# Query and key rows of the dilated heads: eight neighbouring positions to a partition, one load for a head and tensor, and copies that write every second column

## The chip, the cores and the metric

The kernel runs on one core of one Trainium2 chip. The metric is the time of the device in microseconds (us). Five engines take part: TensorE (PE, with its weight loads as PEld), VectorE (DVE), ScalarE (ACT), GpSimd (POOL) and SyncE (SP), whose queue here does nothing but issue loads and stores.

## The reference

Three layers follow each other. Attention over 4 batches, 8 heads, 576 positions and 64 columns a head: the first four heads of a batch look back over 32 neighbouring positions, the last four, the dilated heads, over 32 positions at distance 4. Then a layer of 2048 hidden units with a rational function, then eight experts, each with 1024 hidden units, mixed by a gate that is normalised in turns.

```
rel = pos[:, None] - pos[None, :]
mask_plain = (rel >= 0) & (rel < window)
mask_dil = (rel >= 0) & (rel < window * dilation) & (rel % dilation == 0)
masks = np.stack([mask_plain if h < H // 2 else mask_dil for h in range(H)], axis=0)
scores = np.where(masks[None, :, :, :], scores, -1000000000.0)
...
h = x @ w_in
...
return (g @ w_out).astype(np.float32)
...
out += P[:, e:e + 1] * ye
```

## The kernel before

Attention works on pairs of heads: pair 0 and 1 of a batch are plain, pair 2 and 3 are dilated. For one pair the columns of both heads fill the 128 partitions of `qT` and `kT`, and the 576 positions lie along the free axis. In the dilated pairs the positions are ordered by their remainder by 4, the 144 positions of one remainder behind each other, so that the 32 positions which a query looks at are neighbours. With that order the same code computes plain and dilated pairs.

The way there, for a pair: `att_load` (L266 to L290) loads q and k with positions on the partitions. `att_prep` (L338 to L366) turns them: four steps a pair, x = 0 and 1 for the two halves of q, x = 2 and 3 for those of k; a step is three or four transposes on TensorE into a bank `qkps` (L356) and one copy by ScalarE into `qT` or `kT` (L364), which for a dilated pair also puts the positions in order. `att_qk` adds mask (L372) and products (L379) in a bank `scps`; VectorE takes the maximum (L397), ScalarE three exponentials (L399), VectorE and GpSimd the division (L403 to L405). `att_tr` transposes the result (L414, copy L419), `att_av` multiplies with v (L438), and ScalarE and VectorE split the output into two f16 parts (L229, L232).

For a dilated pair a load of before takes 72 partitions of four neighbouring positions each, that is half of the 576 positions of one head: four loads for q (two heads, two halves) and four for k (L286). In a half the remainder of a position is its place within the partition, and the copy writes runs of 72 neighbouring columns.

Batch 0 is computed first, as a list of pieces (`run_piece`), with other work hung in between (`extra`): the loads and the conversion of the first two column blocks of `w_in` (`wi_load`, L166; `wi_conv`, where ScalarE's L501 is the first to read a loaded piece, then VectorE's L505 to L507 and ScalarE's L536), the scan of v for its maximum (L493), and `wg_prep` (L595), which reads the small load `wgr` (L1324). The second layer begins with the first matmuls L640 to L642. Batches 1 to 3 are worked in pieces between the steps of the second layer.

What sets the order: each engine works through its own queue in order and waits at the first instruction whose inputs are missing. The order itself is made when the program is built, by a list scheduler that works with priorities and with its own estimates of when an input arrives; so a change of a load can move instructions on every engine. SP issues one load after another. Loads carry one of eight counters in turn, and a load waits until the load eight places earlier, with the same counter, has landed.

Of the kernel before, what the change touches and what calls it, by code (L numbers as in the profile page):

```python
# [10 lines left out]
F32 = mybir.dt.float32  # L11
# [17 lines left out]
def kernel(  # L29
# [14 lines left out]
    nc = tc.nc  # L44
    B, H, S, D = q.shape
# [12 lines left out]
    QB = 96  # L58
    KW = 96
    GQ = 192  # L60
    HS = S // 2
    CL = S // 4
    HSTR = S * D
# [47 lines left out]
    def room(tag, shape, dt):  # L111
        where, era, a, size = HOME[tag]
        n = math.prod(shape[1:]) * (2 if dt == F16 else 4)
        assert n <= size, (tag, shape)
        old = rooms.get(where)
        if old is None or old[0] < era:
            old = rooms[where] = era, sb.tile([P, ROOMS[where] // 4], F32R if era == 1 else F32, tag=where, name=f"room{where}")
        assert old[0] == era, (tag, old[0])
        t = old[1][0:shape[0], a // 4:(a + n) // 4]
        if dt != (F32R if era == 1 else F32):  # L120
            t = t.bitcast(dt)
        d = "abcd"[:len(shape) - 1]
        if len(d) > 1:
            t = t.rearrange(f"p ({' '.join(d)}) -> p {' '.join(d)}", **dict(zip(d[1:], shape[2:])))
        return t
# [5 lines left out]
    def bank(name, long=False):  # L131
        bank_n[0] += 1
        if spare_banks[0] and bank_n[0] % 2:
            long = True
        return psum.tile([P, 512], F32, tag="long" if long else "bank", bufs=4, name=name)
# [104 lines left out]
    ident = cpool.tile([P, P], F32, name="ident")  # L240
# [11 lines left out]
    for i, x in enumerate(SEAMS):  # L252
        if x is None:
            continue
        m = masks[:, i, 0:32 + x]
# [11 lines left out]
    def att_load(b, pr, stage=None):  # L267
        off = (b * H + 2 * pr) * HSTR
        st = att.setdefault((b, pr), {})
        if stage:  # L270
            both = room(stage, [P, 2, 1024], F32)
        for i, (src, tag) in enumerate(((q, "aq"), (k, "ak"))):
            if stage:
                w, n = (QB, 6) if pr < 2 else (72, 8)
                t = both[:w, i, 0:n * 2 * D].rearrange("p (c h d) -> p c h d", c=n, h=2)
            elif pr < 2:
                t = room(tag, [QB, 6, 2, D], F32)
            else:
                t = room(tag, [72, 8, 2, D], F32)
            if pr < 2:  # L280
                for h in range(2):
                    nc.sync.dma_start(out=t[:, :, h, :], in_=bass.AP(src.tensor, off + h * HSTR, [[D, QB], [QB * D, 6], [1, D]]))
            else:
                for h in range(2):
                    for y in range(2):
                        nc.sync.dma_start(  # L286
                            out=t[:, 4 * y:4 * y + 4, h, :],
                            in_=bass.AP(src.tensor, off + h * HSTR + y * HS * D, [[4 * D, 72], [D, 4], [1, D]]),
                        )
            st[tag] = t  # L290

    NG = H // 2 * 3

# [36 lines left out]
    def att_qk_tiles(alt):  # L330
        if alt:
            t = room("W3", [P, 2 * S + 32], F32)
            qT, kT = t[:, 0:S], t[:, S:]
        else:
            qT = room("aqT", [P, S], F32)
            kT = room("akT", [P, S + 32], F32)
        nc.vector.memset(kT[:, 0:32], 0.0)
        return qT, kT  # L338

    def att_prep(b, pr, x):  # L340
        st = att[b, pr]
        which, y = divmod(x, 2)
        key = "ak" if which else "aq"
        src = st[key]
        alt = b < 2 and pr % 2
        if x == 0:
            if ("qkT", alt) not in att:
                att["qkT", alt] = att_qk_tiles(alt)
            st["qT"], st["kT"] = att["qkT", alt]
        d = st["kT"][:, 32:] if which else st["qT"]  # L350
        if y == 1:
            st.pop(key)
        w, n = (QB, 3) if pr < 2 else (72, 4)
        bt = bank("qkps")
        for c in range(n):
            nc.tensor.transpose(bt[:, c * w:(c + 1) * w], src[:, n * y + c, :, :].rearrange("p h d -> p (h d)"), ident[:w, :w])  # L356

        def after():
            if pr < 2:
                dv, ps = d[:, y * HS:(y + 1) * HS], bt[:, 0:HS]  # L360
            else:
                dv = d.rearrange("m (c w) -> m c w", c=4)[:, :, y * 72:(y + 1) * 72]
                ps = bt[:, 0:HS].rearrange("m (c p) -> m c p", c=4)
            nc.scalar.activation(dv, ps, AF.Copy, scale=1.0 if which else QSCALE)  # L364

        return after  # L366
# [804 lines left out]
    def run_piece(pc):  # L1171
        kind, b, pr, x = pc
        flush()
        if kind == "prep":
            after.append(att_prep(b, pr, x))
            if x == 3:
                for a in LOADS.get((b, pr), ()):
                    att_load(*a)
        elif kind == "qk":
            after.append(att_qk(b, pr, x))  # L1180
        elif kind == "tr":
            after.append(att_tr(b, pr, x))
        else:
            after.append(att_av(b, pr, x))
            g = b * NG + 3 * pr + x
            if g < 4 or g >= 8:
                att_load_v(g + 8 if g < 4 else g + 4)
# [15 lines left out]
    for b, s0, s1 in ATT:  # L1203
        pcs = att_pieces(b)
        n = 4 * (s1 - s0 + 1) - 4
# [103 lines left out]


    att_load(0, 0)
    for i in range(2):
        att_load_v(i)
    att_load(0, 1, "R1")
    nc.sync.dma_start(out=abt[:, 0:4], in_=ra.partition_broadcast(P))
    nc.sync.dma_start(out=abt[:, 4:6], in_=rb.partition_broadcast(P))
# [16 lines left out]
    n = len(pcs)  # L1333
# [96 lines left out]
```

## Time and profile before

| what | value |
|---|---|
| three runs | 1989.99, 1990.22, 1991.6 us; median 1990.22 us |
| the profiled execution, its own time | 1990.97 us |
| its span in the trace | 1989.0 us |
| TensorE busy | 1892.8 us (95%) |
| VectorE busy | 1574.9 us (79%) |
| ScalarE busy | 1217.4 us (61%) |
| GpSimd busy | 494.5 us (25%) |

The profiled execution lies 0.75 us above the median, and 1.97 us of it lie outside the span. TensorE's busy share is 95% over the whole, but in the page's row of forty slices (49.7 us each) it reads 6 and 6 tenths in the first two, 8 in the third and fourth and 9 from the fifth on, apart from three 8s. The time that TensorE does not work lies mostly at the beginning.

### The profile page before, as it was taken

To read this page: it belongs to the slowest core of one execution; us is meant where nothing else is said; L and a number is where in the kernel's file an instruction comes from. 1 tells how busy PE (TensorE), PEld (TensorE's weight loads), DVE (VectorE), ACT (ScalarE), POOL (GpSimd) and SP (SyncE) were. 2 spreads that over 40 slices of the span, in tenths; PEclk is the share of its full clock that TensorE was granted. 3 is DMA by queue.
4 is the path that set the end of the run, shared out by engine and by line. 5 is a ranking of instruction groups with operands and counts; after the bars stand their busy time and mean duration, and the time that the engine had idled before them with its cause. 6 is when DMAs were issued, how large, how long until landed. Compare 5 with 4: busy or idle time off the path is not lost. (4 is left out here: it accounts for less than half of the span.)

```text
span 1989.0 us, 36639 instructions
## 1 busy us (share of the span) xinstructions
PE 1892.8 (95%) x14202; PEld 1420.9 (71%) x14202; DVE 1574.9 (79%) x2564; ACT 1217.4 (61%) x2182; POOL 494.5 (25%) x489
## 2 busy tenths in 40 slices
PE   6688999999989999999999999999999999999998
PEld 5466676776767677777777777777777777777777
DVE  4696899789997999788778877868877787787764
ACT  4776777776675645656655655555565565565552
POOL 1132234232232104013311411411321141142111
PEclk6689999999999999999999999999999999999999
DMA  6643221124310352465356256335434734543323
GB/s 170 166 139 92 50 71 34 32 63 148 99 43 22 122 172 75 131 176 169 76 119 180 64 118 161 78 82 138 130 60 119 184 65 109 158 93 75 85 59 54
DMA packets 213518, 207.93 MB, mean 105 GB/s; under 512 B 78816, under 2 KB 161248, under 8 KB 213344
## 3 DMA queue, kind: packets, MB, share of 16 engines
q1 hardware_dynamic: 196480, 173.09, 29.2%
q0 software_dynamic: 16864, 32.51, 10.9%
q8 instruction: 111, 1.82, 0.4%
q14 instruction: 63, 0.52, 0.1%
HBM read 155.86 MB, written 49.68 MB: 103 GB/s over the span
## 5 line engine op out<-in xcount | busy, mean ns | idle before, releaser
L930 PEld LDWEIGHTS <-roomA 128*128 128x128 f16 x3276 | 319.6, 98 | 177.1 <-issue 10.1
L930 PE MATMUL l1a<-roomA 128*128 128x384 f16 x1872 | 356.6, 326 | 1.2 <-ACT roomV L979 0.9
L930 PE MATMUL l1b<-roomA 128*128 128x384 f16 x1404 | 273.6, 326 | 3.4 <-DVE roomA L981 1.8
L686 POOL TENSOR_TENSOR roomIG<-roomA,roomIG 128x384 fp32r<-128x384 f32 x96 | 116.4, 1224 | 238.8 <-ACT roomIG L685 217.5
L1030 PE MATMUL yps<-roomA 128*128 128x256 f16 x630 | 169.9, 273 | 2.2 <-DVE roomV L1056 1.5
L1030 PE MATMUL yps<-roomA,roomV 128*128 128x256 f16 x630 | 168.7, 273 | 2.5 <-DVE roomA L1053 1.1
L1031 PE MATMUL yps<-roomA 128*128 128x256 f16 x630 | 170.9, 273 | 0.0
L952 POOL TENSOR_TENSOR roomIG<-roomA 128x384 f32<-128x384 f32 x48 | 60.5, 1260 | 443.9 <-ACT roomA L986 324.9
L1031 PE MATMUL yps<-roomA,roomV 128*128 128x256 f16 x630 | 170.2, 273 | 0.0
L1032 PE MATMUL yps<-roomA 128*128 128x256 f16 x630 | 169.2, 273 | 0.0
L1032 PE MATMUL yps<-roomA,roomV 128*128 128x256 f16 x630 | 168.9, 273 | 0.1
L640 PE MATMUL h1ps<-roomA 128*128 128x384 f16 x384 | 129.2, 336 | 13.0 <-ACT roomA L419 4.1
L701 PE MATMUL o1ps<-roomIG,roomV 128*128 128x384 f32 x384 | 138.9, 362 | 2.7 <-POOL roomIG L686 2.6
L879 POOL TENSOR_TENSOR roomA<-roomA 128x256 f32<-128x256 f32 x140 | 132.5, 966 | 35.6 <-DVE roomA L893 23.8
L702 PE MATMUL o1ps<-roomIG,roomV 128*128 128x384 f32 x384 | 133.1, 347 | 0.0
L893 DVE SCALAR_TENSOR_TENSOR roomA<-roomA,sm 128x768 f16<-128x768 f32 (+1 forms) x92 | 112.4, 1234 | 24.6 <-ACT roomA L890 23.5
L641 PE MATMUL h1ps<-roomA 128*128 128x384 f16 x384 | 129.0, 336 | 0.0
L642 PE MATMUL h1ps<-roomA 128*128 128x384 f16 x384 | 128.8, 335 | 0.0
L952 POOL TENSOR_TENSOR roomIG<-roomV 128x384 f32<-128x384 f32 x48 | 50.4, 1050 | 306.3 <-ACT roomV L986 241.3
L700 PE MATMUL o1ps<-roomIG,roomV 128*128 128x384 f32 x384 | 108.9, 363 | 11.5 <-ACT roomIG L685 10.9
L1030 PEld LDWEIGHTS <-roomA 128*128 128x128 f16 x1008 | 98.7, 98 | 28.6 <-DVE roomA L1056 3.6
L1031 PEld LDWEIGHTS <-roomV 128*128 128x128 f16 x1008 | 98.7, 98 | 25.2 <-issue 2.1
(224 smaller groups left out, 4969.6 us busy)
## 6 DMA issues: line engine op xcount, KB each, us to landing
roomA<-xd SPq DMA_DIRECT2D x119, 384.0 KB
roomA<-in_moe_w_dram SPq DMA_DIRECT2D x256, 128.0 KB
roomA<-in_moe_w_dram SPq DMA_DIRECT2D x128, 256.0 KB
out_dram<-roomV POOLq DMA_DIRECT2D x31, 512.0 KB, 5.8
out_dram<-roomA POOLq DMA_DIRECT2D x31, 512.0 KB, 5.8
roomV<-in_moe_w_in_dram SPq DMA_DIRECT2D x16, 512.0 KB
roomA<-in_moe_w_out_dram SPq DMA_DIRECT2D x16, 512.0 KB
xd<-roomA SPq DMA_DIRECT2D x14, 384.0 KB
```

What stands on the lines that cost most here:

```text
L640: mm = nc.tensor.matmul(hp, whi, xb[:, 0, kk, :], start=kk == 0, stop=False)
L641: nc.tensor.matmul(hp, whi, xb[:, 1, kk, :], start=False, stop=False)
L642: nc.tensor.matmul(hp, wlo, xb[:, 0, kk, :], start=False, stop=kk == KD - 1)
L686: nc.gpsimd.tensor_tensor(out=gl, in0=g, in1=gh.bitcast(F32), op=ALU.subtract)
L701: nc.tensor.matmul(ob[dd], hi, d["gl"], start=False, stop=False)
L702: nc.tensor.matmul(ob[dd], lo, d["gh"], start=False, stop=last)
L879: pin("p" if pool else "v", eng.tensor_tensor(out=d[:, o, :], in0=a, in1=b, op=ALU.add if w == 0 and n == 0 else ALU.subtract))
L893: pin("v", nc.vector.scalar_tensor_tensor(out=l, in0=x, scalar=sc, in1=h, op0=ALU.mult, op1=ALU.subtract))
L930: mm = nc.tensor.matmul(ps, w[:, wx_, wh, kk * P:(kk + 1) * P], x[:, xh, kk, :], start=start and kk == 0 and wh == 0 and xh == 0, stop=sto ...
L1030: nc.tensor.matmul(o, hh[:, a - 1, c], w[:, m, 0, :], start=i == 0 and half == 0, stop=False)
L1031: nc.tensor.matmul(o, hh[:, a - 1, c], w[:, m, 1, :], start=False, stop=False)
L1032: nc.tensor.matmul(o, hl[:, a - 1, c], w[:, m, 0, :], start=False, stop=i == NP - 1 and (last or half == 1 or b == 3))
```

## The change

A partition now holds eight neighbouring positions of a head (position 8p + c on partition p, place c), so one load takes all 576 positions of a head, 72 partitions of 8 times 64 values, and a dilated pair has four loads instead of eight. The two halves of a step are now the places 0 to 3 and 4 to 7. The position 8p + 4y + c has the remainder c and, among those of its remainder, the place 2p + y: the copy of half y therefore writes every second column of `qT` or `kT`, starting at y. Numbers of loaded bytes, transposes and copies stay. The code of plain pairs is written in another way but loads the same pieces.

```
-            if pr < 2:
-                for h in range(2):
-                    nc.sync.dma_start(out=t[:, :, h, :], in_=bass.AP(src.tensor, off + h * HSTR, [[D, QB], [QB * D, 6], [1, D]]))
-            else:
-                for h in range(2):
-                    for y in range(2):
-                        nc.sync.dma_start(
-                            out=t[:, 4 * y:4 * y + 4, h, :],
-                            in_=bass.AP(src.tensor, off + h * HSTR + y * HS * D, [[4 * D, 72], [D, 4], [1, D]]),
-                        )
-            st[tag] = t
+        w, n = (QB, 6) if pr < 2 else (72, 8)
+        rows = [[D, w], [w * D, n], [1, D]] if pr < 2 else [[n * D, w], [D, n], [1, D]]
...
+            for h in range(2):
+                nc.sync.dma_start(out=t[:, h], in_=bass.AP(src.tensor, off + h * HSTR, rows))
+            st[tag] = t.rearrange("p h c d -> p c (h d)")
...
-            nc.tensor.transpose(bt[:, c * w:(c + 1) * w], src[:, n * y + c, :, :].rearrange("p h d -> p (h d)"), ident[:w, :w])
+            nc.tensor.transpose(bt[:, c * w:(c + 1) * w], src[:, n * y + c, :], ident[:w, :w])
...
-                dv = d.rearrange("m (c w) -> m c w", c=4)[:, :, y * 72:(y + 1) * 72]
+                dv = d.rearrange("m (c p y) -> m y c p", c=4, y=2)[:, y]
```

The new order of the instructions differs from the old one on all engines. Below are three places. In the rows of the changed kernel line numbers behind L281 are smaller by 9: L286 and L282 have become L280, L324 L315, L1324 L1315, L364 L355, L399 L390, L419 L410, L501 L492, L536 L527.

SP, the loads for batch 0 behind the last loads of v, up to the first block of `w_in`; the two groups of q and k are those of pair 3. Before:

```order
L324 DMA roomA<-in_v_dram 32x2x64
L324 DMA roomA<-in_v_dram 96x2x64
L1324 DMA wgr<-in_moe_w_gate_dram 128x4x8
L286 DMA roomA<-in_q_dram 72x4x64 x4
L286 DMA roomA<-in_k_dram 72x4x64 x4
L166 DMA roomV_277<-in_moe_w_in_dram 128x1024 x2
L166 DMA roomV_280<-in_moe_w_in_dram 128x1024 x2
```

And now:

```order
L315 DMA roomA<-in_v_dram 32x2x64
L315 DMA roomA<-in_v_dram 96x2x64
L1315 DMA wgr<-in_moe_w_gate_dram 128x4x8
L280 DMA roomA<-in_q_dram 72x8x64 x2
L280 DMA roomA<-in_k_dram 72x8x64 x2
L166 DMA roomV_269<-in_moe_w_in_dram 128x1024 x2
L166 DMA roomV_272<-in_moe_w_in_dram 128x1024 x2
```

Eight issues ahead of the block of `w_in` have become four; the order around them, and up to the second block of `w_in`, is the same.

ScalarE, the end of batch 0, from the split of the gate's weights on (L229 wg) over the four conversions of the first block of `w_in` (L501). Before:

```order
L229 ACTIVATE wg<-wgr,sm 128x4x8
L399 ACTIVATE p,sx<-scps,sx 128x96 x3
L419 ACTIVATE roomA<-ptps 96x384
L399 ACTIVATE roomA,sx<-scps,sx 128x96 x3
L364 ACTIVATE roomV_230<-qkps 128x4x72
L501 ACTIVATE roomV_277<-roomV_277 128x512
L364 ACTIVATE roomV_230<-qkps 128x4x72
```

And now:

```order
L229 ACTIVATE wg<-wgr,sm 128x4x8
L492 ACTIVATE roomV_269<-roomV_269 128x512
L390 ACTIVATE p,sx<-scps,sx 128x96 x3
L410 ACTIVATE roomA<-ptps 96x384
L390 ACTIVATE roomA,sx<-scps,sx 128x96 x3
L355 ACTIVATE roomV_222<-qkps 128x288
L492 ACTIVATE roomV_269<-roomV_269 128x512
```

The first conversion, which waits for a load, has moved ahead of six exponentials, a copy of transposed probabilities (L419) and the first copy of pair 3.

ScalarE again, a little later: the last three triples of exponentials of batch 0 and the first conversions of the second block of `w_in` (L501 with roomV_280). Before:

```order
L399 ACTIVATE roomA,sx<-scps,sx 128x96 x3
L229 ACTIVATE roomA<-avps,sm 128x192
L536 ACTIVATE roomV_280,sm<-roomV_277 128x512 x2
L399 ACTIVATE roomA,sx<-scps,sx 128x96 x3
L419 ACTIVATE roomA<-ptps 96x384 x2
L501 ACTIVATE roomV_280<-roomV_230 128x512
```

And now:

```order
L390 ACTIVATE roomA,sx<-scps,sx 128x96 x3
L492 ACTIVATE roomV_272<-roomV_222 128x512
L229 ACTIVATE roomA<-avps,sm 128x192
L492 ACTIVATE roomV_272<-roomV_222 128x512
L229 ACTIVATE roomA<-avps,sm 128x96
L229 ACTIVATE roomA<-avps,sm 128x48 x2
L410 ACTIVATE roomA<-ptps 96x384
L390 ACTIVATE roomA,sx<-scps,sx 128x96 x3
```

The last triple of exponentials of the batch now stands behind two conversions of the second block.

## Rows read from the trace of the kernel before

**Rows 1.** Busy time by stretch: us of each engine (count), clock, DMA share, GB/s.

```profile
14.00:20.00 6.00, 3.58 (x38) 3.06 (x39) 4.82 (x13) 2.63 (x11) 1.33 (x2) 0.63 1.01 364
20.00:40.00 20.00, 15.02 (x111) 11.59 (x111) 8.87 (x37) 10.71 (x49) 3.48 (x6) 0.50 0.43 90
40.00:70.00 30.00, 18.73 (x162) 13.78 (x163) 16.79 (x55) 18.74 (x62) 2.82 (x5) 0.56 0.78 203
70.00:200.00 130.00, 105.98 (x836) 76.48 (x835) 100.92 (x224) 97.44 (x282) 37.05 (x39) 0.87 0.43 125
```

**Rows 2.** Timeline of SP: start, us, queue, line, out<-in, count.

```profile
10.34 6.02 SPq L286 DMA_DIRECT2D roomA<-in_q_dram  x4
...
16.40 4.38 SPq L286 DMA_DIRECT2D roomA<-in_k_dram  x4
...
31.28 0.46 SPq L1324 DMA_DIRECT2D wgr<-in_moe_w_gate_dram  x1
...
31.79 3.39 SPq L286 DMA_DIRECT2D roomA<-in_q_dram  x4
...
35.22 3.30 SPq L286 DMA_DIRECT2D roomA<-in_k_dram  x4
...
38.64 1.87 SPq L166 DMA_DIRECT2D roomV<-in_moe_w_in_dram  x4
...
50.22 7.22 SPq L324 DMA_DIRECT2D roomA<-in_v_dram  x13
...
57.49 3.23 SPq L166 DMA_DIRECT2D roomV<-in_moe_w_in_dram  x4
...
65.86 4.46 SPq L286 DMA_DIRECT2D roomA<-in_q_dram  x4
...
70.43 3.30 SPq L286 DMA_DIRECT2D roomA<-in_k_dram  x4
```

**Rows 3.** Timeline of TensorE; in brackets the idle time before and its releaser.

```profile
33.52 0.80 PE L180 MATMUL mxps<-ident,sm 128*128 128x128 f32 x2 [2.10 <-DVE sm L595]
...
41.15 0.71 PE L356 MATMUL qkps<-ident,roomA 72*128 72x72 f32 x4 [2.94 <-DMA roomA<-in_k_dram]
...
48.51 2.19 PE L379 MATMUL scps<-roomV 64*64 64x96 f32 x24 [1.17 <-ACT roomV L364]
...
62.83 1.18 PE L438 MATMUL avps<-roomA 96*64 96x64 f32 x12 [4.19 <-ACT roomA L419]
...
69.22 0.50 PE L640 MATMUL h1ps<-roomA 128*128 128x384 f16 x1 [0.98 <-ACT roomA L229]
```

**Rows 4.** Loads by line: ns min/median/max of an issue, first and last start.

```profile
L286 SPq DMA_DIRECT2D roomA<-in_q_dram x32: 790/793/3104, 10.3 to 391.1; - x32
...
L282 SPq DMA_DIRECT2D roomA<-in_q_dram x16: 313/446/1421, 0.8 to 338.7; - x16
...
L313 SPq DMA_DIRECT2D roomA<-in_v_dram x48: 312/416/1528, 3.6 to 382.0; - x48
```

**Rows 5.** Timeline of ScalarE; in brackets the idle time before and its releaser.

```profile
37.54 0.34 ACT L399 ACTIVATE p<-scps,sx 128x96 f32<-128x96 f32 x1 [1.08 <-DVE sx L397]
...
43.64 0.68 ACT L501 ACTIVATE roomV<-roomV 128x512 f32<-128x512 f32 x1 [3.41 <-DMA roomV<-in_moe_w_in_dram]
...
55.96 0.39 ACT L399 ACTIVATE roomA<-scps,sx 128x96 f32<-128x96 f32 x1
...
61.74 0.66 ACT L501 ACTIVATE roomV<-roomV 128x512 f32<-128x512 f32 x1 [3.94 <-DMA roomV<-in_moe_w_in_dram]
...
81.22 0.66 ACT L501 ACTIVATE roomA<-roomA 128x512 f32<-128x512 f32 x1 [2.70 <-DMA roomA<-in_moe_w_out_dram]
```

**Rows 6.** Groups of ScalarE by form: busy us, mean ns, idle before.

```profile
L364 ACT ACTIVATE roomA<-qkps 128x288 f32<-128x288 f32 x48 | 18.6, 412 | 8.9 <-PE qkps L356 8.8
...
L229 ACT ACTIVATE roomA<-avps,sm 128x48 f16<-128x48 f32 x48 | 14.6, 370 | 4.2 <-PE avps L438 4.1
...
L229 ACT ACTIVATE roomA<-avps,sm 128x96 f16<-128x96 f32 x24 | 11.4, 477 | 0.6 <-PE avps L438 0.6
```

More of the change, by code (lines that the diff above doesn't have):

```diff
@@ L271, in att_load @@
             both = room(stage, [P, 2, 1024], F32)
+        w, n = (QB, 6) if pr < 2 else (72, 8)
+        rows = [[D, w], [w * D, n], [1, D]] if pr < 2 else [[n * D, w], [D, n], [1, D]]
         for i, (src, tag) in enumerate(((q, "aq"), (k, "ak"))):
             if stage:
[L274 to L277, printed above, removed]
-            else:
-                t = room(tag, [72, 8, 2, D], F32)
-            if pr < 2:
-                for h in range(2):
-                    nc.sync.dma_start(out=t[:, :, h, :], in_=bass.AP(src.tensor, off + h * HSTR, [[D, QB], [QB * D, 6], [1, D]]))
-            else:
-                for h in range(2):
-                    for y in range(2):
-                        nc.sync.dma_start(
-                            out=t[:, 4 * y:4 * y + 4, h, :],
-                            in_=bass.AP(src.tensor, off + h * HSTR + y * HS * D, [[4 * D, 72], [D, 4], [1, D]]),
-                        )
-            st[tag] = t
+                t = both[:w, i, 0:2 * n * D].rearrange("p (c h d) -> p h c d", c=n, h=2)
+            else:
+                t = room(tag, [w, n, 2, D], F32).rearrange("p c h d -> p h c d")
+            for h in range(2):
+                nc.sync.dma_start(out=t[:, h], in_=bass.AP(src.tensor, off + h * HSTR, rows))
+            st[tag] = t.rearrange("p h c d -> p c (h d)")
     NG = H // 2 * 3
```

## The prediction

> **What bounds the kernel now.** I read the busy shares first, then the forty slices, then the busy time by stretch around the place of the change. TensorE is busy for 95% of the span, so what counts is where it is not. From 70 us on the loss is spread thin: 106.0 of 130 us are busy in 70 to 200 us [rows 1], and what is left behind that is mostly TensorE at work. The beginning is another stage: 15.0 of 20 us are busy in 20 to 40 us and 18.7 of 30 us in 40 to 70 us, both at a granted clock of 0.50 to 0.56, that is near the lower level of 1.2 GHz [rows 1]. The 16.3 us missing in these 50 us are the stage that the change can touch; the rest only inherits the time at which it is left.
>
> Next the timeline of SP. Between 31.28 and 40.51 us it issues without a pause: `wgr`, eight loads for pair 3, four for the first block of `w_in` [rows 2]. The DMA engines are meanwhile busy for 0.43 of the time, against 1.01 in 14 to 20 us, where the scan of v is loaded [rows 1]. So in 20 to 40 us the loads are late because SP issues them late, not because they take long.
>
> Then the waits of TensorE [rows 3]. Three hang on that queue: 2.10 us before 33.52 (L595 on VectorE needs `wgr`), 2.94 us before 41.15 (k of pair 3), and 1.17 us before 48.51 (a copy L364 that stands behind conversions L501, which wait for `w_in`). A fourth is the 4.19 us before 62.83: a copy of ScalarE behind an L501 that waited 3.94 us for the second block of `w_in`, issued at 57.49 [rows 2, 5].
>
> **Part 1: half the issues.** An issue L286 takes 790 ns at its shortest and 793 at the median [rows 4]. What one of 72 x 8 pieces takes the trace does not show. Lower bound 312 ns, the shortest of L313; upper bound 1580, twice L286. L282 moves 576 pieces and L313 288 or fewer, and both have a shortest issue of 312 to 313 ns [rows 4]: the number of pieces does not set it. A nearer row is L286 itself, with the same 72 partitions, so I take 0.83 us with its gap.
>
> Pair 3: eight loads from 31.79 to 38.52 are 6.7 us; four are 3.3. Saved 3.4 us.
>
> Pair 2: eight loads from 10.34 to 20.78 are 10.4 us, where eight at 0.79 would be 6.3. The other 4.1 us are stalls in the issue while the DMA engines are full (1.01) [rows 1, 2]. Halving everything would save 5.2; if the stalls end at fixed moments, when the v loads have drained, nothing. I take 2.0, since most of the stage in question is the full one.
>
> So `wgr` is issued 2.0 us earlier and the first block of `w_in` 5.4 us earlier (bounds 3.4 and 8.6). What is late next:
>
> - The wait before 33.52 falls from 2.10 to 0.1: TensorE gains 2.0.
> - k of pair 3: its third load was out at 37.7 and landed at 41.15, so 3.5 us later. The last of the new four is out at 31.79 + 3.3 - 2.0 = 33.1 and lands at 36.6. TensorE is ready for it at 41.15 - 2.94 - 2.0 = 36.2. The transposes begin at 36.6 instead of 41.15: 4.5 us gained.
> - ScalarE gives some back. The order now puts the first L501 ahead of the exponentials that ran at 37.54 [rows 5]. Its data land 5.0 us after the issue began (38.64 to 43.64), so at 38.2; the exponentials could have run at 35.5. Behind this wait stand six exponentials, a copy L419 and the first copy of pair 3, and TensorE waits for them with the products of v. Going through the row with the durations of before (0.6 an L501 and L536, 1.0 a triple, 0.3 to 0.4 a copy), the last copy of pair 3 starts at about 45 instead of 48.1, just ahead of 48.51: the gain shrinks from 4.5 to 3.0.
> - The second block of `w_in` stands behind thirteen loads of v (7.22 us) that could start only when the first block had landed. It moves with it, by 5.4: its L501 can run at 56.3 instead of 61.74. The last exponentials (55.96 before) now stand behind two L501 and are held until both have data, but the tail of batch 0 that hangs on them lay behind the same data before.
>
> At the first L640 (69.22) the load chain would allow 5.4 and ScalarE's 3.0; both are mixed in that stretch, and I take the middle, 4.2 us.
>
> One rule speaks against all this. The DMA engines stood at 0.43 in 20 to 40 us while SP issued back to back [rows 1, 2]. The Trainium skill, page "DMA: Bandwidth & Descriptors", section "Issuing engines are not separate DMA queues", says that the time to initiate a DMA is usually small relative to the DMA itself; by it part 1 would be worth nothing here. The trace does not agree for this stretch: eight issues take 6.7 us, and a landing follows 3.5 us behind its issue.
>
> **Part 2: the loads of batch 1.** Here pair 2 and 3 of batch 1 have sixteen issues from 65.86 us on, the first eight 7.9 us long [rows 2]. Half of them fall away, and the loads of `w_out` between them come earlier. ScalarE waited 2.70 us at 81.22 for one [rows 5], with work behind it that TensorE needs. I take 1.2 of the 2.70 for TensorE; bounds 0 and 2.7. Later batches load well ahead of use: nothing.
>
> **Part 3: the strided copies.** 32 copies of 288 columns write f32 to every second column, so 8 bytes apart. A contiguous one takes 412 ns [rows 6]. No f32 copy of before writes like this. Nearest are the f16 writes of L229, also 8 bytes apart: 48 columns take 370 ns, 96 take 477, so 2.23 ns a column. At that rate 288 columns take 370 + 240 x 2.23 = 905 ns, 0.49 more. Lower bound 0: the same values are read and written, and no row shows a spread write gaining. I take the middle, 0.25 us. In batch 0 two copies of pair 3 stand directly before scores that TensorE waits for: 0.5 us. The 24 of later batches lie beside a TensorE that has matmuls of the second layer in its queue: 24 x 0.25 = 6.0 us of ScalarE, of which I let 0.2 through. If this cover were gone, it would be all 6.0.
>
> The L229 rows show 2.23 ns a column at 8 bytes apart. The Trainium skill, page "SBUF — State Buffer", section "Door 1: The DMA port swizzle", says that accesses run at full bandwidth while there are two hits to a line of 16 bytes; two columns of 8 bytes are two hits, so the copies would cost nothing and the sum would be 0.7 lower. The L229 rows disagree, if their f16 is no special case.
>
> **Part 4: the new order.** TensorE has the same instructions, but queues differ in places through the second layer. TensorE lost 24 us in 70 to 200 [rows 1]; I take 0 and allow 3 us either way, the clock included, since 0.87 was granted there and other gaps may move its steps.
>
> Sum: -4.2 - 1.2 + 0.5 + 0.2 = -4.7 us. On the profiled execution, 1990.97 us (span 1989.0 and 1.97 around it), that is 1986.3. The median lies 0.75 lower, so I predict 1985.5 us.
>
> **Rivals.**
>
> - Given back: the stalls of pair 2 are fixed in time (saving 0, the block of `w_in` lands at 40.2), and ScalarE holds the exponentials from about 37.5 until then, so most of the gain at 41.15 is lost. For it: full DMA engines until 20 us. Against it: the wait at 62.83 still shrinks with the second block. It leaves about -1.7: 1988.5.
> - All of it: SP is the bound and the stalls halve too. 8.6 earlier for `w_in`, no wait for ScalarE: -8.6 - 1.2 + 0.7 = -9.1, 1981.
> - Slower, ScalarE: the copies cost the full 0.49 and the engine's queue is held for it, on ScalarE just ahead of scores. 32 x 0.49 = 15.7, less 5.4 gained, is +10.3 in the extreme; with batch 0's eight in full (3.9) and half of the other 24 (5.9) it is 1990.2 - 5.4 + 9.8 = 1994.6. It turns from gain to loss where copies cost 0.17 us each on the path (5.4 / 32). Against it: ScalarE is busy for 97 of 130 us in 70 to 200 [rows 1].
> - Slower, the change doesn't do what it says: an issue of twice the pieces takes twice the 0.79. Nothing comes earlier, but the order is built for early data: the L501 still gets its data at 43.64, the exponentials of 37.54 wait behind it for 6 us, and TensorE's products of v at 41.8 move to about 46. 1990.2 + 4.3 + 0.7 = 1995. Against it: L282 and L313 [rows 4].
>
> **How the numbers follow.** About 0.2%, 4 us, is what a measurement of this kernel can tell from no change: faster is under 1986.2, slower over 1994.2. The forecast has 0.47, its own range 1982 to 1989 by the bounds 3.4 and 8.6, 0 and 2.7 and the order; two thirds of it are under 1986.2. Given back 0.23, nearly all within; all of it 0.13, faster; the slow copies 0.10 and the doubled issue 0.07, together 0.14 over the bound and the rest within. Faster 0.48, same 0.38, slower 0.14. The range reaches from 1979 (all of it, with 2 us of luck in the order) to 1995.
>
> **What would show it.** Right: SP's four loads of pair 3 end near 33 us and the first block of `w_in` begins there; no wait of TensorE for `wgr`; the first L640 near 65; an issue of 72 x 8 near 0.8 us; copies of 0.41 to 0.66 us. Wrong: an issue near 1.6 us; L501's wait near 38 us over 3 us long; copies of 0.9 us with TensorE waiting for them; a gain at the first L640 that is gone by 200 us, which would put the blame on the order or the clock.

## The result and the profile after

The changed kernel takes 1974.88 us in the median of four runs (1973.71 to 1978.19), the kernel before beside it 1990.91; the ratio is 0.991, 95% interval 0.9891 to 0.9929. The medians lie 16 us apart, where 4.7 were forecast, and the measured time is 4 us under the range. Its profiled execution is the longest of the four, with a span of 1976.1 us.

SyncE's timeline answers to [rows 2] (start, us, queue, line, names, count):

```profile
29.27 0.45 SPq L1315 DMA_DIRECT2D wgr<-in_moe_w_gate_dram  x1
29.76 1.72 SPq L280 DMA_DIRECT2D roomA<-in_q_dram  x2
31.53 1.63 SPq L280 DMA_DIRECT2D roomA<-in_k_dram  x2
33.28 2.12 SPq L166 DMA_DIRECT2D roomV<-in_moe_w_in_dram  x4
...
52.82 1.87 SPq L166 DMA_DIRECT2D roomV<-in_moe_w_in_dram  x4
```

The load of `wgr` leaves 2.0 us earlier (29.27 against 31.28), pair 3's four loads take 3.5 us to the next start where eight took 6.85, and w_in's first block leaves 5.4 us earlier (33.28 against 38.64), the second 4.7.

The loads of pair 3 answer to [rows 4] (ns shortest/median/longest; over the whole program line L280 holds the plain heads too), and the copies to [rows 6] (mean ns):

```profile
L280 SPq DMA_DIRECT2D roomA<-in_q_dram x2: 825/837/849, 29.8 to 30.7; - x2
L280 SPq DMA_DIRECT2D roomA<-in_k_dram x2: 792/792/792, 31.5 to 32.4; - x2
```

```profile
L355 ACT ACTIVATE roomA<-qkps 128x288 f32<-128x288 f32 x48 | 19.3, 424 | 10.0 <-PE qkps L347 9.6
```

An issue of 72 x 8 pieces takes what one of 72 x 4 took: over all 32 dilated loads 792 ns at the shortest and 800 in the median, against 790 and 791 over the 64 of before. The copies of this row, half of which belong to plain pairs and are contiguous as before, last 424 ns in the mean instead of 412.

TensorE's timeline answers to [rows 3], ScalarE's to [rows 5] (in brackets the idle time before and its releaser):

```profile
31.48 0.79 PE L180 MATMUL mxps<-ident,sm 128*128 128x128 f32 x2 [1.02 <-DVE sm L586]
36.86 0.71 PE L347 MATMUL qkps<-ident,roomA 72*128 72x72 f32 x4 [0.69 <-DMA roomA<-in_k_dram]
...
58.76 0.85 PE L405 MATMUL ptps<-ident,roomA 128*96 128x128 f32 x3 [6.08 <-DVE roomA L232]
...
68.93 0.50 PE L631 MATMUL h1ps<-roomA 128*128 128x384 f16 x1
```

```profile
38.72 0.66 ACT L492 ACTIVATE roomV<-roomV 128x512 f32<-128x512 f32 x1 [4.30 <-DMA roomV<-in_moe_w_in_dram]
...
57.17 0.66 ACT L492 ACTIVATE roomV<-roomV 128x512 f32<-128x512 f32 x1 [5.95 <-DMA roomV<-in_moe_w_in_dram]
```

Pair 3's transposes begin 4.3 us earlier (36.86 against 41.15), and ScalarE stands at its first L492 for 4.30 us with the exponentials behind it, as the changed order made one expect. Yet the second layer's first matmul comes only 0.3 us earlier, 68.93 against 69.22: TensorE waits 6.08 us before 58.76, and in the new order more of batch 0 stands between that wait and this matmul (60 products of v, against 12 behind the wait of 4.19 before). Matched matmul by matmul, the lead over the kernel before (median of 20 us) is 8 us at 110 us, 7 at 200 to 240, between 8 and 12 from 320 to 580, 16 at 630 and 13.5 at the end. Two orders can't be compared by such marks: while they mix attention and second layer differently, one instruction may be early and another late. So the time to TensorE's last matmul is split by what it was lost to: waits (TensorE idle), and time at 1.2 GHz (half of TensorE's busy time in stretches that the profile grants 1.2). What remains is between 1846 and 1851 us in every profile of this study. In us:

| profile | 0 to 300: waits, 1.2 GHz | 300 to 660: waits, 1.2 GHz | from 660 | remains | last matmul ends |
|---|---|---|---|---|---|
| before | 53.1, 34.9 | 21.7, 8.0 | 13.8 | 1849.9 | 1981.4 |
| after | 47.9, 33.3 | 17.9, 4.6 | 15.7 | 1848.5 | 1967.9 |

Before lost 88.0 us until 300 us and 29.7 until 660, the changed kernel 81.2 and 22.5. Half of this gain (6.8 us) lies where the loads were expected to bring it, half (7.2) behind it.

### The profile page after: what moved, and what is told of

Same layout as the page of the kernel before. It is cut to its first block, busy times and chain, and to the rows that moved or that the text cites. A ratio compares the mean times of both kernels' runs of the same rounds, so it can differ in the third digit from the quotient of the medians.

```text
span 1976.1 us, 36600 instructions
## 1 busy us (share of the span) xinstructions
PE 1886.4 (95%) x14202; PEld 1418.3 (72%) x14202; DVE 1567.5 (79%) x2564; ACT 1217.0 (62%) x2182; POOL 491.1 (25%) x489
## 5 line engine op out<-in xcount | busy, mean ns | idle before, releaser
L692 PE MATMUL o1ps<-roomIG,roomV 128*128 128x384 f32 x384 | 136.2, 355 | 4.0 <-POOL roomIG L677 3.8
L884 DVE SCALAR_TENSOR_TENSOR roomA<-roomA,sm 128x768 f16<-128x768 f32 (+1 forms) x92 | 114.5, 1257 | 24.7 <-ACT roomA L881 23.9
L693 PE MATMUL o1ps<-roomIG,roomV 128*128 128x384 f32 x384 | 130.6, 340 | 0.0
L691 PE MATMUL o1ps<-roomIG,roomV 128*128 128x384 f32 x384 | 107.5, 363 | 15.9 <-ACT roomIG L676 15.8
L881 ACT ACTIVATE roomA<-roomA,sm 128x768 f16<-128x768 f32 (+1 forms) x92 | 93.7, 1035 | 37.4 <-POOL roomA L870 17.8
```

The lines of the kernel that those rows point to most:

```text
L692: nc.tensor.matmul(ob[dd], hi, d["gl"], start=False, stop=False)
L693: nc.tensor.matmul(ob[dd], lo, d["gh"], start=False, stop=last)
L884: pin("v", nc.vector.scalar_tensor_tensor(out=l, in0=x, scalar=sc, in1=h, op0=ALU.mult, op1=ALU.subtract))
```

## The experiments

Three theories stood at first. A: the loads bring some 7 us, the new order of the instructions the rest. B: the loads bring all. C: the order brings all. To part them, the order was fixed by a table, one list for each engine (in short form):

```
+    for order in table:                       # one for each engine
+        for a, b in zip(order, order[1:]):
+            tc.add_manual_dep(b, a.name, NoSync)    # place in the queue, no wait
```

No run has a kernel with nothing but its own order as table; the nearest is m1, with two pieces exchanged, which took 1974.8 us where the changed kernel took 1974.9. What the expectations call the first layer is the layer of w_in and w_out. All runs, with the time lost in the profiled execution of each (waits and 1.2 GHz together). The ratio is to the kernel before, timed beside each run. The profiled execution is often a long one: p4's took 1980.7 and c1's 1986.6, so the lost time of these two is that of an execution 8 and 4 us over the median.

| run | loads | order | median us | ratio to before | lost until 300 | 300 to 660 |
|---|---|---|---|---|---|---|
| before | two a head | old | | 1 | 88.0 | 29.7 |
| x1 | one | old | 1984.9 | 0.9957 [0.9943, 0.9972] | 80.9 | 30.0 |
| c1 | two, gapped | old | 1983.0 | 0.9949 [0.9933, 0.9965] | 80.4 | 30.6 |
| x2 | two | new | 1982.5 | 0.9944 [0.9929, 0.9959] | 86.4 | 24.7 |
| p1 | two | third | 1981.6 | 0.9937 [0.9919, 0.9954] | 84.4 | 27.0 |
| p2 | two | fourth | 1984.9 | 0.9952 [0.9936, 0.9969] | 88.5 | 25.7 |
| after | one | new | 1974.9 | 0.991 [0.9891, 0.9929] | 81.2 | 22.5 |
| after, again | one | new | 1972.4 | 0.9895 [0.988, 0.991] | 80.2 | 22.1 |
| e4 | two, gapped | new | 1975.6 | 0.9908 [0.9888, 0.9927] | 81.9 | 22.1 |
| h1 | one | new to 69 us, old | 1985.1 | 0.9961 [0.9946, 0.9976] | 82.3 | 30.8 |
| h5 | one | old to 464 us, new | 1984.8 | 0.9963 [0.9948, 0.9978] | 82.8 | 32.2 |
| h4 | one | old to 285 us, new | 1973.8 | 0.9904 [0.9889, 0.992] | 80.5 | 25.4 |
| p3 | one | its third | 1981.5 | 0.994 [0.9924, 0.9955] | 79.8 | 30.4 |
| p4 | one | its fourth | 1972.5 | 0.99 [0.988, 0.992] | 80.6 | 27.2 |
| m1 | one, w_in first | new | 1974.8 | 0.9903 [0.988, 0.9925] | 77.6 | 24.4 |
| b2 | one, w_in first | as h4 | 1976.3 | 0.9915 [0.9901, 0.9929] | 79.0 | 24.7 |

### Loads against order

x1 is the changed kernel with the table of the kernel before.

> The changed kernel (one load for a head and tensor, copies to every second column), with the instructions of each engine fixed in the order in which the kernel before has them (of two loads that are now one, the place of the first). Theory A (the merged loads bring w_in some 5 us earlier, which is worth 6 to 7 us; the rest of the gain is the new order of the instructions on TensorE, ScalarE and VectorE): 1984, between 1981 and 1987. Rival B (the loads carry all of it): 1975, as the changed kernel. Rival C (the new order carries all of it): 1990, as the kernel before.

x2 is the kernel before with the table of the changed one.

> The kernel before (two loads for a head and tensor, plain copies), with the instructions of each engine fixed in the order in which the changed kernel has them (two loads in the place of the one). Theory A: 1983, between 1979 and 1987: the start is as late as before, the later gain of 7 to 9 us is kept. Rival B: 1990. Rival C: 1975.

Both came where A has them, 1984.9 and 1982.5, with intervals that exclude 1 and the changed kernel's 0.991. The loads are worth 0.0043 in the old order (8.6 us) and 0.0034 in the new (6.8), the order 0.0056 with the old loads (11.1) and 0.0047 with the new (9.4 us). So each brings about the same with the other as without it; the 0.0009 between is within the intervals. The lost time says the same: the loads change the column until 300 us (88.0 to 80.9, 86.4 to 81.2), the order that behind it (29.7 to 24.7, 30.0 to 22.5). In x1 the second layer starts 6.4 us earlier than before [rows 3], and the lead stays between 4.5 and 9.3 us (medians of 20 us) to the end:

```profile
62.85 0.48 PE L631 MATMUL h1ps<-roomA 128*128 128x384 f16 x1 [0.83 <-ACT roomA L229]
```

### The copies alone, and the form of the source

```
-in_=bass.AP(src.tensor, off + h * HSTR + y * HS * D, [[4 * D, 72], [D, 4], [1, D]])
+in_=bass.AP(src.tensor, off + h * HSTR + y * 4 * D, [[8 * D, 72], [D, 4], [1, D]])
-dv = d.rearrange("m (c w) -> m c w", c=4)[:, :, y * 72:(y + 1) * 72]
+dv = d.rearrange("m (c p y) -> m y c p", c=4, y=2)[:, y]
```

> The kernel before with the copies of q and k of the dilated heads to every second column alone: eight neighbouring positions in a partition, but still fetched by two DMAs of four positions for a head and tensor; the order of the instructions is that of the kernel before. Theories A, B and C alike: 1991, within 2 us of the kernel before, since the copies last 0.015 us more. A rival by which the strided copies change the time (0.25 to 0.5 us each, as forecast): 1993 to 1996.

It took 1983.0, which none of the theories had: as much gained as with half the loads. SyncE's loads of c1, by line and in the timeline:

```profile
L286 SPq DMA_DIRECT2D roomA<-in_q_dram x32: 300/414/2587, 10.3 to 382.6; - x32
```

```profile
30.48 1.86 SPq L286 DMA_DIRECT2D roomA<-in_q_dram  x4
32.39 1.81 SPq L286 DMA_DIRECT2D roomA<-in_k_dram  x4
34.33 1.77 SPq L166 DMA_DIRECT2D roomV<-in_moe_w_in_dram  x4
```

Eight loads take 3.85 us to the next start, where before eight took 6.85 and the changed kernel's four 3.5; an issue takes 0.41 in the median against 0.79 before [rows 4], with the same 72 x 4 pieces to the same places. The pieces do not differ either: the traces of before, of c1 and of the changed kernel all have 61824 packets of 256 bytes in the first 420 us. What differs is the source: before, a load read 288 rows that are one run in DRAM; here it reads four rows of every eight. That gave a new theory, D: what costs is the form of the source, not the number of loads. e4 is c1's edit with the table of the changed kernel.

> The changed kernel, but each head's load of eight neighbouring positions cut in two again (the first four and the last four of each eight: 8 loads of 72x4 rows for a pair, as many as before, whose rows in DRAM have gaps), in the order of the instructions of the changed kernel (two loads in the place of the one). Theory D (what the change saves is not the number of loads but the form of their source: 72x4 rows with gaps took 0.46 us of issue each in the run of the copies alone, 72x4 rows that are one run in DRAM 0.85, 72x8 that are one run 0.82, so eight gapped halves cost as little as four whole heads): 1975, within 2 us of the changed kernel, with w_in's first block issued at 33 to 34.5 us. Rival (it takes one load in place of two): 1982.5, as the kernel before in the new order, with w_in's first block at 38 us.

```profile
L286 SPq DMA_DIRECT2D roomA<-in_q_dram x32: 306/413/3141, 10.3 to 380.4; - x32
```

```profile
30.82 1.86 SPq L286 DMA_DIRECT2D roomA<-in_q_dram  x4
32.73 1.82 SPq L286 DMA_DIRECT2D roomA<-in_k_dram  x4
34.67 1.77 SPq L166 DMA_DIRECT2D roomV<-in_moe_w_in_dram  x4
```

1975.6: D holds. One load in place of two is one way to an earlier w_in, and the layout with eight positions read by as many loads as before is another, as good. Why a source in one run takes 0.79 us to issue is open. A merged load with gaps was not tried.

### w_in ahead of pair 3

The changed kernel with its own table, in which on SyncE two pieces change places:

```
 wgr <- moe_w_gate
+w_in, first block (4 loads)
 q and k of pair 3 (4 loads)
-w_in, first block (4 loads)
```

> The changed kernel in its own order, except that SyncE issues the four loads of w_in's first block ahead of the four loads of pair 3. If the direct half of the gain comes because w_in's first block is issued earlier (33.3 us instead of 38.6): it goes out 3.3 us earlier still, at about 30, and 2 to 3 us more are won: 1972. If the loads of q and k are what counts in that stage: they go out 1.9 us later, TensorE's 0.69 us wait for k of pair 3 becomes 2.6: 1977. If neither: 1975.

1974.8, the same as the changed kernel within the intervals. SyncE, ScalarE's first L492, and TensorE:

```profile
30.09 1.84 SPq L166 DMA_DIRECT2D roomV<-in_moe_w_in_dram  x4
31.98 1.73 SPq L280 DMA_DIRECT2D roomA<-in_q_dram  x2
33.75 4.74 SPq L280 DMA_DIRECT2D roomA<-in_k_dram  x2
```

```profile
34.80 0.67 ACT L492 ACTIVATE roomV<-roomV 128x512 f32<-128x512 f32 x1 [0.19 <-DMA roomV<-in_moe_w_in_dram]
```

```profile
40.63 0.71 PE L347 MATMUL qkps<-ident,roomA 72*128 72x72 f32 x4 [4.75 <-DMA roomA<-in_q_dram]
42.35 0.72 PE L347 MATMUL qkps<-ident,roomA 72*128 72x72 f32 x4 [1.00 <-DMA roomA<-in_k_dram]
```

ScalarE's wait of 4.30 us is gone (0.19), and TensorE waits 4.75 us for q of pair 3 instead: both blocks are wanted at once.

### Is the order chance?

p1 and p2 are the kernel before in two other orders that the scheduler finds for it after a trifle has changed; p3 and p4 are the changed kernel with the like. The trifles, of which only the table is kept (the first line stands twice for p1 and p3, the second moves for p2 and p4):

```
+nc.sync.dma_start(out=abt[:, 0:4], in_=ra.partition_broadcast(P))    # twice: p1, p3
...
-nc.sync.dma_start(out=wgr, in_=w_gate.rearrange("(k p) e -> p k e", p=P))
 att_load(0, 3, "R3")
+nc.sync.dma_start(out=wgr, in_=w_gate.rearrange("(k p) e -> p k e", p=P))    # p2, p4
```

> The kernel before, with nothing changed but the order of the instructions: it is the one that the scheduler finds when one more small load (2 KB, left out again here) stands among the first loads; 440 of 2022 places differ on ScalarE, 536 of 2564 on VectorE, 1235 of 13591 on TensorE. Theory A1 (which order comes out is chance, and any two orders of this kernel can lie some 8 us apart): anywhere from 1981 to 1999, and this or the next run more than 3 us from the kernel before. Rival A2 (the new order is better for a reason that comes with the earlier loads): within 2 us of 1991.

> The kernel before, in the order that the scheduler finds when the load of the gate's weights (16 KB) stands behind the loads of pair 3: SyncE issues it 7 us later, 434 places differ on ScalarE, 521 on VectorE, 1207 on TensorE. Theory A1: anywhere from 1981 to 1999. Rival A2: within 2 us of 1991.

> The changed kernel in an order that the scheduler finds for it when one more small load (2 KB, left out again here) stands among the first loads; 643 of 2022 places differ from the changed kernel's order on ScalarE, 795 of 2564 on VectorE, 2584 of 13591 on TensorE. Theory A1 (chance decides which order comes out, and the change drew a good one): 1976 to 1986, and this and the next run together later than the changed kernel, about 1980. Rival A3 (the order of the kernel before is the only bad one; any other does as well): 1975, within 2 us of the changed kernel.

> The changed kernel in the order that the scheduler finds for it when the load of the gate's weights (16 KB) stands behind the loads of pair 3; 668 places differ on ScalarE, 822 on VectorE, 3049 on TensorE. Theory A1: 1976 to 1986. Rival A3: within 2 us of 1975.

A1 holds for the spread: the same work of the old kernel lies at 1, 0.9944, 0.9937 and 0.9952 in four orders, that of the changed one at 0.9957, 0.991, 0.994 and 0.99. The old kernel had the worst of its four, the changed kernel one of its two best. A3 falls by p3 (0.994). The means of the fours, 0.9958 and 0.9927, are 0.0031 apart, 6.2 us; the third and fourth orders are not the same for both, so this is a rough figure of what the change itself brings.

### Where and how the order works

h1 has the new order until the second layer's first matmul, h4 and h5 the old one until two later points (in short form):

```
+table = new[:n] + [i for i in old if i not in new[:n]]    # h1
+table = old[:n] + [i for i in new if i not in old[:n]]    # h4, h5
```

> The changed kernel; up to the first matmul of the first layer (68.9 us) each engine has the changed kernel's order, after that what is left has the order of the kernel before. Theory A, with the order's share in the later part: 1984, 1981 to 1987 (as the changed loads in the old order). If the order's share lies in the first 69 us: 1975. Rival B: 1975.

> The changed kernel; each engine keeps the order of the kernel before until ScalarE's 600th instruction (285 us in the changed kernel's trace) and has the changed kernel's order from there. The old order throughout gave 1985, the new one 1975. If the 9 us of the order are won where TensorE's lead over the old order grows in the traces (1 us until 300 us, 3 to 5 more until 550, the rest until 640): 1976 to 1977. If they are spread evenly over the first 640 us: 1979 to 1980. If they hang on the start: 1985.

> As the run before, but the old order is kept until ScalarE's 900th instruction (464 us in the changed kernel's trace). By the lead in the traces (4 us of 9 won by then): 1979. Spread evenly: 1982. If what matters is the end of the first layer alone (580 to 640 us): 1976.

1985.1, 1973.8, 1984.8: the new order is not needed before 285 us and brings nothing if it begins after 464. So places between are needed, where batch 3 of attention (in the changed kernel its products of v run from 365 to 454 us) is worked between the steps of the second layer; whether those behind 464 are needed as well was not tried. A mixed order is also an order of its own, and each cut was made once: that h4 drew a good one and h5 a bad one by chance is not excluded. h5 refutes the even spread and the reading of the lead. Two more profiles of x1 and of the changed kernel, which took 1979.8 and 1983.7 us and 1972.7 and 1973.2, were to show how.

> The changed loads in the old order, profiled once more. TensorE's time to its last matmul is split in three: busy at 2.4 GHz (1848.5 in all kernels, within 2), lost at 1.2 GHz (half of its busy time in stretches granted 1.2 GHz; 41.9 in the first profile), and waits (82.5). Theory W (the order works through waits): its waits lie 5 us or more above those of the changed kernel in its own order. Theory K (through the clock): waits within 3 us of it, the loss at 1.2 GHz 4 to 8 us above. Theory N (the split is the execution's, not the order's): the loss varies within this kernel by as much as between the two.

> The changed kernel, profiled once more; in the first profile 37.8 us lost at 1.2 GHz and 81.6 of waits. Theory W: waits 77 or less. Theory K: loss 34 to 38, waits about 82. Theory N: loss anywhere from 36 to 50.

> The changed loads in the old order, a third profile of the same kernel; the theories W, K and N expect of it what they expect of the second one.

> The changed kernel, a third profile of the same kernel; the theories W, K and N expect of it what they expect of the second one.

One row each of the busy times from 300 to 660 us (TensorE, its weight loads, VectorE, ScalarE, GpSimd, each with its count; granted clock; DMA), x1, x1_b, x1_c, then the changed kernel, after_b, after_c:

```profile
300.00:660.00 360.00, 336.24 (x2307) 257.10 (x2306) 319.75 (x488) 252.32 (x489) 102.49 (x86) 0.98 0.22 65
```

```profile
300.00:660.00 360.00, 340.43 (x2306) 260.78 (x2307) 318.69 (x489) 251.84 (x488) 102.35 (x86) 0.97 0.22 66
```

```profile
300.00:660.00 360.00, 339.15 (x2300) 259.90 (x2299) 318.24 (x487) 251.58 (x488) 102.40 (x86) 0.97 0.21 65
```

```profile
300.00:660.00 360.00, 342.12 (x2367) 262.53 (x2366) 323.62 (x501) 257.85 (x494) 102.01 (x88) 0.98 0.24 72
```

```profile
300.00:660.00 360.00, 340.69 (x2365) 261.59 (x2364) 323.37 (x500) 256.54 (x492) 100.72 (x88) 0.99 0.24 72
```

```profile
300.00:660.00 360.00, 340.78 (x2363) 261.09 (x2361) 323.20 (x500) 257.44 (x494) 101.83 (x88) 0.99 0.24 72
```

In x1_b and after_b TensorE is busy for the same 340 us, and the second does 59 matmuls more: the clock stands at 0.99 instead of 0.97. Split as above, x1 loses 6.2, 11.0 and 10.8 us to 1.2 GHz in this stretch and waits 23.8, 19.6 and 20.9; the changed kernel loses 4.6, 2.9 and 2.9 and waits 17.9, 19.3 and 19.2.

In the mean that is 9.3 against 3.5 and 21.4 against 18.8: 5.9 us by the clock, 2.6 by waits, together 8.5 of the 9.4. The sum is the firm part: 30.0 to 31.7 in x1, 22.1 to 22.5 in the changed kernel, a fourth profile (the one beside b2) included. How it divides varies more: x1's own loss to the clock goes from 6.2 to 11.0. The other two pairs of old and new order, one profile each, have 4.0 by the clock and 1.0 by waits (before, x2), and 4.7 and 3.8 (c1, e4).

So in this stretch K is nearest, with some of W, but the stretch was chosen after the fact. As they were stated, for the whole program, W's waits of 77 or less came (75.9 and 74.4) but not its difference of 5 us (means of 80.5 and 77.3), K's loss of 34 to 38 did not (38.3 and 41.6), and N is not refuted (losses of 41.9, 41.4, 47.7 in x1 against 37.8, 38.3, 41.6). Which of the moved instructions keeps the clock up between 285 and 464 us was not found.

### The early w_in in the better order

b2 is h4 with the swap of m1; the changed kernel was timed beside it once more.

> The kernel of the old order until 285 us and the new one from there (1973.75), with w_in's first block issued ahead of pair 3's loads as well. If w_in's first block is what the start waits for: 2 to 3 us less, 1971, and 3 to 4 less than the changed kernel. If what the start wins is given back by 285 us: 1974, as the changed kernel. If pair 3's loads, 1.9 us later, are what it waits for: 1976.

> The changed kernel once more, timed on the same chip as b2: 1975, and 0.991 of the kernel before. Its place is to say how far b2 and the changed kernel lie apart when both are timed together.

1976.3 against 1972.4: nothing won. No version tried is shown to be faster than the changed kernel.

## Why the prediction was wrong

- Part 1, SyncE: right. `wgr` 2.0 us and w_in's first block 5.4 us earlier, as worked out; four issues of 72 x 8 pieces in 3.5 us where 3.3 was taken; pair 3's transposes at 36.9 where 36.6 was forecast. TensorE's wait for `wgr` fell from 2.10 to 1.02 us, not to 0.1. "All of it" and "given back" differ in SyncE's stalls of pair 2, and the middle was measured; that the 2.0 us taken between 0 and 5.2 fit so well is luck. ScalarE's hold behind the first L492 came too, and at 4.30 us it is over the 3 that were named as a sign of being wrong; yet until 300 us the new order lost about as much as the old one (81.2 against 80.9 in x1). The second layer's first matmul, named as a sign of being right near 65 us, came at 68.93 in the new order, in which more of batch 0 had moved ahead of it, and at 62.85 in the old one.
- Its worth was set too low: 4.2 us at the second layer's first matmul, where x1, which has the order that the forecast started from, has 6.4; with the copies and batch 1 a sum of 4.7, where the loads are worth 8.6 in the old order and 6.8 in the new. Until 300 us 88.0 us were lost before and 80.9, 79.3 and 80.3 in x1's three profiles. That x1's 1984.9 is so near the forecast of 1985.5 is luck: the kernel before took 1993.3 beside x1, and 1990.2 in the runs that the forecast started from, so x1's gain is 8.4 us and not 4.7.
- Part 2, batch 1: one wait of ScalarE for `w_out`, 2.70 us, was counted, and 1.2 of it taken. From 66 to 110 us ScalarE waited 5.2 us for `w_out` before and 0.5 in x1, where TensorE's lead grows from 6.4 to 9.3 us by 110 us. So at that place the term was too small as well; how much of it lasts is not shown, for the lead falls again to between 5 and 8.
- The reason given was too narrow: the sum counted loads. It was right that neither pieces nor, as the rival of the doubled issue had it, their doubling sets the issue time; but nor does the number of loads as such (c1, e4). [rows 4] pointed to it: L282 and L313, whose pieces do not follow each other in DRAM in the order of the load, at 416 to 446 ns beside L286 at 793.
- Part 3, the copies: 0.25 us each was taken and about 0.02 measured (12 ns in the mean over 48, 24 of which are changed; matched copy by copy in the same order, the 32 changed ones last 430 ns in x1 and 411 before, the others 415 in both). The f16 writes of L229 were the wrong row to go by. The Trainium skill, page "SBUF — State Buffer", section "Door 1: The DMA port swizzle", by which two hits to a line of 16 bytes run at full bandwidth, is nearer the measurement than those writes: 430 against 411 ns, 5% and not nothing. The rival of the slow copies falls.
- **Part 4 is the step that failed:** "I take 0 and allow 3 us either way", with no more reason for the 0 than that TensorE has the same instructions. The order is worth 9 to 11 us, and the profiles have it in TensorE's waits and time at 1.2 GHz between 300 and 660 us (30.0 to 31.7 us lost in x1, 22.1 to 22.5 in the changed kernel). Nor was its place right: 70 to 200 us was looked at. Four orders of the old kernel spread over 0.0063, 12.5 us, so 3 us were far too few. Why this order is the better one stays open.
- The chances do not follow from their parts: two thirds of 0.47, all of 0.13 and none of the rest make 0.44 for faster and leave 0.42 for same, where 0.48 and 0.38 were given.
- The Trainium skill, page "DMA: Bandwidth & Descriptors", section "Issuing engines are not separate DMA queues", by which the time to initiate a DMA is usually small relative to the DMA itself, would have made part 1 worth nothing; x1 and c1 measure 8.6 and 10 us. One issue is small here too, 0.79 us against the 3.5 to its landing; it is the eight behind each other that cost.

## What to carry to other kernels

Where a scheduler makes the order, a small edit draws a new one, and this alone moved this kernel by up to 12 us; to learn what the edit itself brings, fix the order of before and measure the edit in it, or measure both in several orders. Compare orders by TensorE's lost time (waits, and time at the lower clock), not by when one instruction runs. Where a queue issues back to back, look at the issue time of each form of load before merging loads: here a different split of the rows did as well as half the loads.

## What was not expected of the hardware

- A load of 72 x 4 pieces of 256 bytes takes SyncE 793 ns to issue in the median when its source is one run in DRAM [rows 4], and 414 ns when the source has gaps (c1), with the same destination and the same packets; one run of twice the pieces takes 792 at the shortest and 800 in the median. Why is not shown.
- A copy of 288 f32 columns to every second column is about 0.02 us slower than one to runs of 72 (430 against 411 ns).
- TensorE's time without waits and without the loss at 1.2 GHz is the same within 4.1 us (1846.4 to 1850.5) in twenty profiles, whatever the order.
